# Splitting the weights of the matmul stage on VectorE and ScalarE alone, with two load buffers held by both stages

## The chip, the core and the metric

The kernel runs on one core of a Trainium2 chip. TensorE (PE in the profile) does the matmuls, VectorE (DVE), ScalarE (ACT) and GpSimd (POOL) the elementwise work, and SyncE (SP) issues all loads and stores from one queue, in order. The metric is the device time of one execution in microseconds (us); lower is better.

## What is computed

The reference is an attention with a memory term, followed by two gated feed-forward layers:

```python
a = softmax(causal(q @ k.T / 8))
local = a @ v
mem_out = (phi(q) @ M_prev) / (phi(q) @ z_prev + 1e-6)     # phi(x) = elu(x) + 1
x = g * mem_out + (1 - g) * local                          # g = sigmoid(beta), per head
x = (sigmoid(x @ w_gate) * (x @ w_val)) @ w_out            # layer 0
x = ((x @ w_a) * (x @ w_b)) @ w_out2                       # layer 1
```

q, k, v are 4 x 8 x 576 x 64, so the layers see 2304 tokens of width 512; the hidden width is 1536. Inputs of the kernel and all weights are taken as float64 words: each weight arrives as two 32-bit halves.

## The kernel before

Every float32 operand of a matmul is kept as a high and a low part of type fp32r, and every product is three matmuls into one PSUM sum (`mm3`, lines 501 to 503: high by high, high by low, low by high). The hidden width is cut into 12 chunks (`NCH`) of 128. A chunk of a layer has three weight pieces, gate, value and output (`kind` 0, 1, 2), and each piece must be brought from 64-bit words into a high and a low tile before TensorE can use it. `w_piece` does that for one piece: a load of 512 KB into a buffer `st`, then the split, in three steps between its `yield`s. `w_stream` runs pieces one behind the other and issues loads ahead.

The kernel has two stages. The first, to about 357 us of the profile, is the attention, with the layer-0 matmuls of chunks 0 to 3 (`MA`) for three of the four batches woven in (`moe_a`); it also splits the 15 pieces of chunks 0 to 4 (`KA`). A scheduler orders the instructions of all engines there. The second is the matmul stage. There TensorE's order is the program's; the other engines are still ordered by the scheduler. `run` goes over the chunks of one block of tokens: for chunk c, `gv` does 24 matmuls (gate and value sums), then 12 matmuls of the chunk before, `outs`, follow. Between them lies `gate`: DVE multiplies (L579, it reads PSUM), ACT writes the high part `gh` (L149), GpSimd the low part `gl` (L585), and `outs` of that chunk needs both. The blocks go in this order: layer 0, batch 3, all 12 chunks; layer 0, the 256 left-over tokens (blk = 4); layer 0, batches 0 to 2, chunks 4 to 11; then layer 1. Weight pieces are split under these blocks: 21 pieces (chunks 5 to 11 of layer 0) under the first, 12 pieces of layer 1 under batch 0, 24 under batch 2 and the first block of layer 1. `w_steps(k)` runs k steps of the stream at each chunk, placed behind the last gate instruction by `tc.issue_after`.

In the matmul stage a piece costs DVE six instructions (L415, L419, L420, L434, L439, L448), ACT one (L416) and GpSimd one multiplication (L424), which stands between them: L439 reads what L424 writes. Three buffers `st` take the loads, in memory that the first stage gives back.

Of the kernel before, what the change touches and what calls it, by code (L numbers as in the profile page):

```python
# [12 lines left out]
ALU = mybir.AluOpType  # L13
# [6 lines left out]
def kernel(  # L20
# [38 lines left out]
    wp = ctx.enter_context(tc.tile_pool(name="wp", bufs=KA))  # L59
    xsp = ctx.enter_context(tc.tile_pool(name="xsp", bufs=4))  # L60

    lctx, rctx = ExitStack(), ExitStack()
# [338 lines left out]
    def w_piece(wsrc, layer, c, kind, src):  # L401
        s = work.tile([P, 512, 2], I32, tag="st", name="st", bufs=NST)
        w32 = wsrc[kind].bitcast(I32)
        if kind == 2:
            nc.sync.dma_start(out=s.rearrange("p f t -> p (f t)"), in_=w32[c * P:(c + 1) * P, :])
        else:
            nc.sync.dma_start(
                out=s.rearrange("p (a f) t -> p a (f t)", a=KD),
                in_=w32[:, 2 * c * P:2 * (c + 1) * P].rearrange("(a p) f -> p a f", p=P),
            )  # L410
        yield
        hi, lo = s[:, :, 1], s[:, :, 0]
        top = work.tile([P, 512], I32, tag="wt", name="wt", bufs=NW)
        low = work.tile([P, 512], I32, tag="wl", name="wl", bufs=1)
        vec.tensor_scalar(out=top, in0=hi, scalar1=0x7FFFFE00, scalar2=None, op0=ALU.bitwise_and)  # L415
        act.activation(out=top, in_=top, func=AF.Relu, scale=8.0, bias=rebias)  # L416
        yield
        t = src.tile([P, 2, 512], F32R, tag=f"w{kind}", name=f"w{kind}")
        vec.tensor_scalar(out=low, in0=hi, scalar1=0x1FF, scalar2=None, op0=ALU.bitwise_and)  # L419
        vec.tensor_scalar(  # L420
            out=hi, in0=hi, scalar1=-(1 << 31), scalar2=0x3F800000, op0=ALU.bitwise_and,
            op1=ALU.bitwise_or,
        )
        pool.tensor_tensor(  # L424
            out=t[:, 0], in0=top.bitcast(F32), in1=hi.bitcast(F32), op=ALU.mult
        )
        if WPOOL:
            act.activation(out=low.bitcast(F32), in_=low, func=AF.Copy, scale=2.0 ** -20)
            vec.scalar_tensor_tensor(
                out=low.bitcast(F32), in0=lo.bitcast(U32), scalar=2.0 ** -52, in1=low.bitcast(F32),  # L430
                op0=ALU.mult, op1=ALU.add,
            )
        else:
            vec.scalar_tensor_tensor(  # L434
                out=low.bitcast(F32), in0=low, scalar=2.0 ** 32, in1=lo.bitcast(U32),
                op0=ALU.mult, op1=ALU.add,
            )
        yield
        vec.tensor_scalar(  # L439
            out=top, in0=t[:, 0].bitcast(I32), scalar1=-(1 << 23), scalar2=None,  # L440
            op0=ALU.bitwise_and,
        )
        if WPOOL:
# [3 lines left out]
        else:  # L447
            vec.scalar_tensor_tensor(  # L448
                out=t[:, 1], in0=low.bitcast(F32), scalar=2.0 ** -52, in1=top.bitcast(F32),
                op0=ALU.mult, op1=ALU.mult,  # L450
            )
        ws[layer, c, kind] = t
        yield

    def w_stream(pieces, ahead, skew=False):

        gens = []  # L460
        pieces = iter(pieces)

        def more():
            a = next(pieces, None)
            if a is not None:
                g = w_piece(*a)
                next(g)
                gens.append(g)

        for _ in range(ahead):  # L470
            more()
        yield
        old = None
        if skew and gens:
            next(gens[0])
            yield
        while gens:
            g = gens.pop(0)
            if skew:
                if old:  # L480
                    next(old)
                    yield
                if gens:
                    next(gens[0])
                    yield
                next(g)
                more()
                yield
                old = g
                continue  # L490
# [5 lines left out]
        if old:  # L496
            next(old)
            yield

# [232 lines left out]
    w1, w2_ = (w1g, w1v, w1o), (w2a, w2b, w2o)  # L732
    NST, NG, NW = 2, MA, 1
    CD = "q"
    EDVE = ""
    WPOOL = True
    if True:
        start()
        wst = w_stream(
            [(w1, 0, c, kind, wp) for kind in range(3) for c in range(MA)]  # L740
            + [(w1, 0, c, kind, wp) for c in range(MA, KA) for kind in range(3)], 2
        )
        batches = list(range(B - 1))
        cur, deferred, finished, cut_a = [], [], [], []
# [40 lines left out]
        def fill(p):  # L785
            settle()
            split(1)
            if p >= 1:
                with tc.issue_after(st["pace"].ins):
                    for _ in range(1 if p < 4 else 2):  # L790
                        next(wst, None)

        def room(p):

            old = divmod(p - 4, NPAIR)
            while any(x[1] is split_a and x[2] == old for x in split_q):
                split(1)
                if not M():
                    next(wst, None)

# [99 lines left out]
        while cur or batches or split_q or deferred:  # L900
            M()
            fill(NP)
        for _ in wst:
            pass
    rctx.close()
    lctx.close()
    with tc.manual_schedule(engines={mybir.EngineType.PE}):
# [5 lines left out]
        psb = bctx.enter_context(tc.tile_pool(name="psb", bufs=4, space=bass.MemoryType.PSUM))  # L913
        NST, NG, NW = 3, 2, 2
        WPOOL = False
        wst = w_stream(
            [(w1, 0, c, kind, w2) for c in range(KA, NCH) for kind in range(3)], NST, True
        )

        def w_steps(k):  # L920
# [30 lines left out]
        every, upper = list(range(NCH)), list(range(MA, NCH))  # L951
        run(0, B - 1, every, lambda m: w_steps(9), (0, B))
        w_steps(1000)
        run(0, B, every, lambda m: None, (0, 0))
        for blk in range(B - 1):
            last = blk == B - 2
            if blk == 0:
                wst = w_stream(
                    [(w2_, 1, c, kind, wp) for c in range(MA) for kind in range(3)], NST, True
                )  # L960
            if last:
# [4 lines left out]
                        for c in range(MA, NCH) for kind in range(3)  # L966
                    ], NST, True
# [39 lines left out]
```

## Time and profile before

| | |
|---|---|
| time, 3 runs | 1184.41, 1187.15, 1188.86 us; median 1187.15 |
| profiled execution | 1186.88 us, of which the span is 1185.1 |
| busy in the span | PE 1136.8, DVE 560.2, ACT 446.5, POOL 435.8 us |
| TensorE's granted clock | 0.991 of full on the mean |

The page cuts the span into 40 slices of 29.6 us and gives the busy tenths of each engine. In this kernel PE is at nine tenths or more from the sixth slice to the end, but for one place, the slices around 420 to 470 us. A busy share says little of a stage in which PE does all that it can; what matters here is where PE waits, and for whom.

### The profile page before, as it was taken

The numbers are of one execution on the slowest core, as the hardware profiler recorded it, in microseconds if no ns is written. First come the engines' busy times: TensorE is split into PE (matmuls) and PEld (weight loads), VectorE is DVE, ScalarE is ACT, GpSimd is POOL, SyncE is SP. The second block draws the span as 40 slices with busy tenths as digits, with TensorE's granted clock in tenths as the row PEclk, the third lists the DMA queues.
The fourth block names the chain that finished last, engine by engine and source line by source line (L and its number), as shares of the span: only waits on it lengthen the run. The fifth ranks groups of instructions, "written<-read, shape, count | busy, mean of one in ns | idle before, by whom it ended". The sixth has DMA issues, their size and how long they took to land. (4 is left out here: it accounts for less than half of the span.)

```text
span 1185.1 us, 16296 instructions
## 1 busy us (share of the span) xinstructions
PE 1136.8 (96%) x6088; PEld 928.6 (78%) x6088; DVE 560.2 (47%) x1233; ACT 446.5 (38%) x985; POOL 435.8 (37%) x387
## 2 busy tenths in 40 slices
PE   5889899999999987999999999999999999999998
PEld 4667677787878865998888887878888888888897
DVE  6899988655636776127721579741100200200111
ACT  5877767777743222132312223222211211211221
POOL 5777776453413553124421254431111111111111
PEclk9999999999999998999999999999999999999999
DMA  7454443342114333014420334401000200100000
GB/s 172 111 154 107 131 118 109 77 112 76 46 50 150 122 107 120 36 53 135 134 89 10 132 107 131 154 18 36 36 1 1 72 1 1 51 8 1 5 37 18
DMA packets 130816, 89.67 MB, mean 76 GB/s; under 512 B 90417, under 2 KB 118065, under 8 KB 129841
## 3 DMA queue, kind: packets, MB, share of 16 engines
q1 hardware_dynamic: 130736, 88.63, 25.9%
q8 instruction: 48, 0.79, 0.3%
q14 instruction: 32, 0.25, 0.1%
HBM read 71.31 MB, written 17.30 MB: 75 GB/s over the span
## 5 line engine op out<-in xcount | busy, mean ns | idle before, releaser
L585 POOL TENSOR_TENSOR gl<-sg,gh 128x512 fp32r<-128x512 f32 (+1 forms) x120 | 145.9, 1216 | 506.4 <-ACT gh L149 480.4
L501 PE MATMUL gv<-xs,w 128*128 128x512 f32 (+1 forms) x864 | 320.0, 370 | 5.8 <-POOL w L424 5.2
L503 PE MATMUL gv<-xs,w 128*128 128x512 f32 (+1 forms) x864 | 320.0, 370 | 3.3 <-DVE w L448 3.3
L502 PE MATMUL gv<-xs,w 128*128 128x512 f32 (+1 forms) x864 | 319.7, 370 | 1.6 <-DVE xs L644 1.6
L579 DVE TENSOR_TENSOR sg<-gv,sg 128x512 f32<-128x512 f32 (+1 forms) x108 | 68.1, 630 | 417.0 <-PE gv L503 408.0
L501 PEld LDWEIGHTS gv<-xs,w 128*128 128x128 f32 x864 | 163.5, 189 | 37.2 <-POOL w L424 7.0
L503 PEld LDWEIGHTS gv<-xs,w 128*128 128x128 f32 x864 | 163.6, 189 | 33.9 <-DVE w L448 5.3
L502 PEld LDWEIGHTS gv<-xs,w 128*128 128x128 f32 x864 | 163.5, 189 | 31.9 <-DVE xs L644 2.7
L424 POOL TENSOR_TENSOR w<-wt,st 128x512 fp32r<-128x512 f32 x72 | 114.6, 1591 | 120.2 <-ACT wt L416 59.2
L149 ACT ACTIVATE gh<-sg 128x512 fp32r<-128x512 f32 (+1 forms) x120 | 70.5, 588 | 215.1 <-DVE sg L579 215.0
L666 ACT ACTIVATE sg<-gv 128x512 f32<-128x512 f32 (+1 forms) x108 | 59.0, 547 | 238.9 <-PE gv L503 234.8
L416 ACT ACTIVATE wt<-wt,rebias 128x512 int32<-128x512 int32 x72 | 51.9, 723 | 128.4 <-DVE wt L415 128.3
L247 ACT ACTIVATE s<-s,mx 128x320 f32<-128x320 f32 (+3 forms) x128 | 78.0, 610 | 24.6 <-DVE mx L242 23.7
L698 PE MATMUL mo<-w,gl 128*128 128x512 f32 x216 | 85.2, 395 | 1.5 <-POOL gl L585 1.4
L696 PE MATMUL mo<-w,gh 128*128 128x512 f32 x216 | 84.9, 393 | 0.0
L697 PE MATMUL mo<-w,gh 128*128 128x512 f32 x216 | 84.8, 393 | 0.0
L149 ACT ACTIVATE aw<-tp 128x512 f32<-128x512 f32 (+1 forms) x144 | 70.5, 508 | 27.5 <-PE tp L328 23.0
L502 PE MATMUL mo<-gl,w 128*128 128x512 f32 (+1 forms) x192 | 70.5, 367 | 1.5 <-POOL gl L585 1.5
L242 DVE CUSTOM_DVE_ANT_0 s<-sc,mask 64x64 f32<-64x64 f32 (+4 forms) x144 | 62.2, 470 | 17.9 <-PE sc L217 17.7
L501 PE MATMUL mo<-gh,w 128*128 128x512 f32 (+1 forms) x192 | 70.2, 366 | 0.0
L503 PE MATMUL mo<-gh,w 128*128 128x512 f32 (+1 forms) x192 | 70.2, 366 | 0.0
L439 DVE TENSOR_SCALAR wt<-w 128x512 int32<-128x512 int32 x72 | 36.2, 502 | 48.5 <-POOL w L424 48.5
(108 smaller groups left out, 1814.8 us busy)
## 6 DMA issues: line engine op xcount, KB each, us to landing
st<-in_moe_w_out_dram SPq DMA_DIRECT2D x24, 512.0 KB, 3.6
kn<-in_k_dram SPq DMA_DIRECT2D x64, 128.0 KB, 2.8
st<-in_moe_w_gate_dram SPq DMA_DIRECT2D x12, 512.0 KB, 3.7
st<-in_moe_w_val_dram SPq DMA_DIRECT2D x12, 512.0 KB, 3.8
st<-in_moe_w_a_dram SPq DMA_DIRECT2D x12, 512.0 KB, 3.6
st<-in_moe_w_b_dram SPq DMA_DIRECT2D x12, 512.0 KB, 3.5
xd<-x SPq DMA_DIRECT2D x16, 288.0 KB, 2.7
qn<-in_q_dram SPq DMA_DIRECT2D x32, 128.0 KB, 2.8
```

Source lines behind the costliest of these rows:

```text
L149: act.activation(out=out, in_=src, func=AF.Copy)
L242: st["pace"] = vec.tensor_tensor_reduce(out=s, in0=sc[0:m, SC0[i]:SC0[i] + w], in1=mask[0:m, c:c + w], scale=1.0, scalar=BIG, op0=ALU.add, ...
L247: act.activation(out=o, in_=s, func=AF.Exp, scale=-1.0, bias=mx[0:m, i:i + 1], accum_out=sm[0:m, i:i + 1],)
L424: pool.tensor_tensor(out=t[:, 0], in0=top.bitcast(F32), in1=hi.bitcast(F32), op=ALU.mult)
L501: pe.matmul(o, lhsT=w[:, 0, ws_], rhs=xh, start=first, stop=False, skip_group_check=True)
L502: pe.matmul(o, lhsT=w[:, 0, ws_], rhs=xl, start=False, stop=False, skip_group_check=True)
L503: pe.matmul(o, lhsT=w[:, 1, ws_], rhs=xh, start=False, stop=last, skip_group_check=True)
L579: st["gate"] = vec.tensor_tensor(out=s[:, 0:n], in0=vps[:, 0:n], in1=s[:, 0:n], op=ALU.mult)
L585: pool.tensor_tensor(out=gl[:, 0:n], in0=s[:, 0:n], in1=gh[:, 0:n].bitcast(F32), op=ALU.subtract)
L696: pe.matmul(mo[f], lhsT=gh[:, t], rhs=w[:, 0], start=first, stop=False)
L697: pe.matmul(mo[f], lhsT=gh[:, t], rhs=w[:, 1], start=False, stop=False)
L698: pe.matmul(mo[f], lhsT=gl[:, t], rhs=w[:, 0], start=False, stop=c == NCH - 1)
```

## The change

The load buffers `st` get a pool of their own, `stp`, with two buffers, which lives through both stages. The weight stream of the first stage is not closed at its end: its list now holds the 21 pieces of chunks 5 to 11 too, and a counter (`left`) stops it after 46 steps, so that loads of the next two pieces are issued in the first stage, and the matmul stage goes on with the same stream. In the matmul stage GpSimd's multiplication is gone. The DVE instructions of a piece are now: **top** (L417, upper bits), **low** (L420, low bits), **low sum** (L446), **sign** (L452, one instruction that puts the sign bit to the rescaled top), **cut** (L456, the power of two, written into `st`) and **second** (L459, the low tile, which reads `st`). ACT has two: the rescaling (L418) and, new, a copy of `top` that writes the high tile (L455). The order of steps by pairs (`skew`) is gone, and `w_steps` takes 6 steps at a chunk where it took 9. The first stage's split is as before.

```diff
+    stp = ctx.enter_context(tc.tile_pool(name="stp", bufs=2))
...
-        s = work.tile([P, 512, 2], I32, tag="st", name="st", bufs=NST)
+        s = stp.tile([P, 512, 2], I32, tag="st", name="st")
...
-        t = src.tile([P, 2, 512], F32R, tag=f"w{kind}", name=f"w{kind}")
         vec.tensor_scalar(out=low, in0=hi, scalar1=0x1FF, scalar2=None, op0=ALU.bitwise_and)
-        vec.tensor_scalar(
-            out=hi, in0=hi, scalar1=-(1 << 31), scalar2=0x3F800000, op0=ALU.bitwise_and,
-            op1=ALU.bitwise_or,
-        )
-        pool.tensor_tensor(
-            out=t[:, 0], in0=top.bitcast(F32), in1=hi.bitcast(F32), op=ALU.mult
-        )
...
+        vec.scalar_tensor_tensor(
+            out=low.bitcast(F32), in0=low, scalar=2.0 ** 32, in1=lo.bitcast(U32),
+            op0=ALU.mult, op1=ALU.add,
+        )
+        yield
+        t = (src or w2).tile([P, 2, 512], F32R, tag=f"w{kind}", name=f"w{kind}")
+        vec.scalar_tensor_tensor(
+            out=top, in0=hi, scalar=-(1 << 31), in1=top, op0=ALU.bitwise_and, op1=ALU.bitwise_or
+        )
+        act.activation(out=t[:, 0], in_=top.bitcast(F32), func=AF.Copy)
+        vec.tensor_scalar(
+            out=hi, in0=top, scalar1=-(1 << 23), scalar2=None, op0=ALU.bitwise_and
+        )
+        vec.scalar_tensor_tensor(
+            out=t[:, 1], in0=low.bitcast(F32), scalar=2.0 ** -52, in1=hi.bitcast(F32),
+            op0=ALU.mult, op1=ALU.mult,
+        )
         ws[layer, c, kind] = t
         yield
...
-            + [(w1, 0, c, kind, wp) for c in range(MA, KA) for kind in range(3)], 2
-        )
+            + [(w1, 0, c, kind, wp if c < KA else None) for c in range(MA, NCH) for kind in range(3)],
+            2,
+        )
+        left = [1 + 9 * KA]
...
-        wst = w_stream(
-            [(w1, 0, c, kind, w2) for c in range(KA, NCH) for kind in range(3)], NST, True
-        )
...
-        run(0, B - 1, every, lambda m: w_steps(9), (0, B))
+        run(0, B - 1, every, lambda m: w_steps(6), (0, B))
...
-                    [(w2_, 1, c, kind, wp) for c in range(MA) for kind in range(3)], NST, True
+                    [(w2_, 1, c, kind, wp) for c in range(MA) for kind in range(3)], 2
...
-            run(0, blk, upper, (lambda m: 1 < m < 7 and w_steps(9)) if last else
+            run(0, blk, upper, (lambda m: 1 < m < 7 and w_steps(6)) if last else
...
-            run(1, blk, every, lambda m: w_steps(9), (1, order[i + 1]) if i < B else None)
+            run(1, blk, every, lambda m: w_steps(6), (1, order[i + 1]) if i < B else None)
```

TensorE's order of instructions is the same in both kernels, and so is the order on DVE, ACT and GpSimd in the whole first stage. Two places of the matmul stage differ in what the prediction rests on.

The first is DVE's queue in the first block, before. The rows begin with the gate of chunk 2 (`sg<-gv,sg`); twelve weight rows stand between it and the gate of chunk 3, of which eleven are shown (w_4750 and w_4763 are tiles of two pieces).

```order
L579 TENSOR_TENSOR sg<-gv,sg 128x512
L439 TENSOR_SCALAR wt<-w_4750 128x512
L448 SCALAR_TENSOR_TENSOR w_4750<-wl,wt 128x512
L415 TENSOR_SCALAR wt<-st 128x512
L419 TENSOR_SCALAR wl<-st 128x512
L420 TENSOR_SCALAR st<-st 128x512
L434 SCALAR_TENSOR_TENSOR wl<-wl,st 128x512
L439 TENSOR_SCALAR wt<-w_4763 128x512
L448 SCALAR_TENSOR_TENSOR w_4763<-wl,wt 128x512
L415 TENSOR_SCALAR wt<-st 128x512
L419 TENSOR_SCALAR wl<-st 128x512
L420 TENSOR_SCALAR st<-st 128x512
```

The same place after the change, from the gate of chunk 1 on (L568 is the gate now).

```order
L568 TENSOR_TENSOR sg<-gv,sg 128x512
L417 TENSOR_SCALAR wt<-st 128x512
L420 TENSOR_SCALAR wl<-st 128x512
L446 SCALAR_TENSOR_TENSOR wl<-wl,st 128x512
L452 SCALAR_TENSOR_TENSOR wt<-st,wt 128x512
L417 TENSOR_SCALAR wt<-st 128x512
L456 TENSOR_SCALAR st<-wt 128x512
L459 SCALAR_TENSOR_TENSOR w_4749<-wl,st 128x512
L452 SCALAR_TENSOR_TENSOR wt<-st,wt 128x512
L420 TENSOR_SCALAR wl<-st 128x512
L446 SCALAR_TENSOR_TENSOR wl<-wl,st 128x512
L456 TENSOR_SCALAR st<-wt 128x512
```

No row waits for GpSimd's tile any more (before, L439 reads `w`). Between two gates there now stand 14 weight rows, not 12: 5, 7, 14, 14, 13, 14, 14, 13, 14, 12 and 6 rows ahead of the gates of chunks 0 to 10. The last row of a piece (L459) frees its `st` for the load of the piece after the next.

The second place is SP's queue at the start of the matmul stage. Before, the first three pieces are loaded here, ahead of the loads `xt` of the left-over tokens:

```order
L407 DMA st<-in_moe_w_gate_dram 128x4x256
L407 DMA st<-in_moe_w_val_dram 128x4x256
L405 DMA st<-in_moe_w_out_dram 128x1024
L636 DMA xt<-xd_94 128x64
L636 DMA xt<-xd_95 128x64
```

After, the first two pieces have been loaded in the first stage, and the third stands behind ten loads `xt`, the last four of which are shown:

```order
L625 DMA xt<-xd_99 128x64
L625 DMA xt<-xd_100 128x64
L625 DMA xt<-xd_97 128x64
L625 DMA xt<-xd_98 128x64
L407 DMA st<-in_moe_w_out_dram 128x1024
L625 DMA xt<-xd_99 128x64
L625 DMA xt<-xd_100 128x64
L409 DMA st<-in_moe_w_gate_dram 128x4x256
```

The third piece has moved behind the ten small loads, and the first two are gone from here.

## Rows read from the trace of the kernel before

**Rows 1.** The page: its span, and the busy row of part 1.

```profile
span 1185.1 us, 16296 instructions
...
PE 1136.8 (96%) x6088; PEld 928.6 (78%) x6088; DVE 560.2 (47%) x1233; ACT 446.5 (38%) x985; POOL 435.8 (37%) x387
```

**Rows 2.** Windows: length, busy by engine, granted clock, DMA share, GB/s.

```profile
420.00:440.00 20.00, 17.78 (x75) 13.48 (x73) 14.81 (x28) 5.13 (x8) 10.54 (x7) 1.00 0.34 106
440.00:460.00 20.00, 12.27 (x42) 7.67 (x42) 15.99 (x29) 4.64 (x7) 9.24 (x6) 0.87 0.36 108
...
452.00:456.00 4.00, 1.04 (x3) 0.59 (x3) 3.36 (x5) 0.63 (x1) 2.82 (x2) 0.87 0.41 127
456.00:460.00 4.00, 1.80 (x4) 0.62 (x3) 2.73 (x7) 0.72 (x1) 1.66 (x1) 0.50 0.19 53
```

**Rows 3.** Waits of PE, 335 to 480 us: total, times, longest.

```profile
PE gv L501 <- POOL w L424: 5.2, 4, 2.2
PE gv L503 <- DVE w L448: 3.3, 3, 1.4
```

**Rows 4.** Timeline of PE: start, duration; first matmuls of three groups.

```profile
370.58 0.39 PE L501 MATMUL gv<-xs,w 128*128 128x512 f32 x1
...
378.74 0.39 PE L501 MATMUL gv<-xs,w 128*128 128x512 f32 x1
...
469.57 0.28 PE L501 MATMUL gv<-xs,w 128*128 128x256 f32 x1
```

**Rows 5.** Timeline of DVE, one round in the first block; idle time in brackets.

```profile
414.77 0.69 DVE L579 TENSOR_TENSOR sg<-gv,sg 128x512 f32<-128x512 f32 x1
...
416.52 1.67 DVE L448 SCALAR_TENSOR_TENSOR w<-wl,wt 128x512 fp32r<-128x512 f32 x1
418.22 0.43 DVE L415 TENSOR_SCALAR wt<-st 128x512 int32<-128x512 int32 x1
418.56 0.42 DVE L419 TENSOR_SCALAR wl<-st 128x512 int32<-128x512 int32 x1
419.02 0.43 DVE L420 TENSOR_SCALAR st<-st 128x512 int32<-128x512 int32 x1
419.36 0.69 DVE L434 SCALAR_TENSOR_TENSOR wl<-wl,st 128x512 f32<-128x512 int32 x1
421.25 0.43 DVE L439 TENSOR_SCALAR wt<-w 128x512 int32<-128x512 int32 x1 [1.20 <-POOL w L424]
421.71 0.69 DVE L448 SCALAR_TENSOR_TENSOR w<-wl,wt 128x512 fp32r<-128x512 f32 x1
422.44 0.43 DVE L415 TENSOR_SCALAR wt<-st 128x512 int32<-128x512 int32 x1
...
424.18 0.68 DVE L579 TENSOR_TENSOR sg<-gv,sg 128x512 f32<-128x512 f32 x1
```

**Rows 6.** Timelines of ACT and POOL behind the gate at 414.77.

```profile
415.55 0.63 ACT L149 ACTIVATE gh<-sg 128x512 fp32r<-128x512 f32 x1 [1.33 <-DVE sg L579]
...
416.26 1.38 POOL L585 TENSOR_TENSOR gl<-sg,gh 128x512 fp32r<-128x512 f32 x1 [0.23 <-ACT gh L149]
```

**Rows 7.** Loads: two rows of SP's timeline, and st's landings, 360 to 470 us.

```profile
360.74 0.38 SPq L407 DMA_DIRECT2D st<-in_moe_w_gate_dram  x1
...
362.26 6.13 SPq L636 DMA_DIRECT2D xt<-xd  x9
...
DMA to landing us min/median/max: 3.4/3.6/5.9
```

**Rows 8.** Windows of the later blocks, columns as in Rows 2.

```profile
520.00:600.00 80.00, 80.00 (x363) 65.71 (x362) 54.77 (x96) 25.20 (x42) 33.69 (x22) 1.00 0.39 119
...
716.00:796.00 80.00, 76.39 (x325) 60.23 (x324) 60.43 (x101) 21.79 (x35) 36.58 (x24) 1.00 0.34 106
```

**Rows 9.** A gate of layer 1, after the last piece is split.

```profile
798.94 0.69 DVE L579 TENSOR_TENSOR sg<-gv,sg 128x512 f32<-128x512 f32 x1 [7.67 <-PE gv L503]
```

**Rows 10.** Landings of st in the first stage, 150 to 210 us.

```profile
DMA to landing us min/median/max: 3.6/4.8/6.1
```

More of the change, by code (lines that the diff above doesn't have):

```diff
@@ L417, in w_piece @@
         yield
-        t = src.tile([P, 2, 512], F32R, tag=f"w{kind}", name=f"w{kind}")
         vec.tensor_scalar(out=low, in0=hi, scalar1=0x1FF, scalar2=None, op0=ALU.bitwise_and)
-        vec.tensor_scalar(
-            out=hi, in0=hi, scalar1=-(1 << 31), scalar2=0x3F800000, op0=ALU.bitwise_and,
-            op1=ALU.bitwise_or,
-        )
-        pool.tensor_tensor(
-            out=t[:, 0], in0=top.bitcast(F32), in1=hi.bitcast(F32), op=ALU.mult
-        )
-        if WPOOL:
+        if WPOOL:
+            t = src.tile([P, 2, 512], F32R, tag=f"w{kind}", name=f"w{kind}")
+            vec.tensor_scalar(
+                out=hi, in0=hi, scalar1=-(1 << 31), scalar2=0x3F800000, op0=ALU.bitwise_and,
+                op1=ALU.bitwise_or,
+            )
+            pool.tensor_tensor(
+                out=t[:, 0], in0=top.bitcast(F32), in1=hi.bitcast(F32), op=ALU.mult
+            )
             act.activation(out=low.bitcast(F32), in_=low, func=AF.Copy, scale=2.0 ** -20)
@@ L432, in w_piece @@
             )
[L433 to L436, printed above, removed]
-            )
[L438 to L441, printed above, removed]
-        )
-        if WPOOL:
+            yield
+            vec.tensor_scalar(
+                out=top, in0=t[:, 0].bitcast(I32), scalar1=-(1 << 23), scalar2=None,
+                op0=ALU.bitwise_and,
+            )
             pool.tensor_tensor(
@@ L446, in w_piece, with w_stream @@
             )
[L447 to L450, printed above, removed]
-            )
+            ws[layer, c, kind] = t
+            yield
+            return
+        vec.scalar_tensor_tensor(
+            out=low.bitcast(F32), in0=low, scalar=2.0 ** 32, in1=lo.bitcast(U32),
+            op0=ALU.mult, op1=ALU.add,
+        )
+        yield
+        t = (src or w2).tile([P, 2, 512], F32R, tag=f"w{kind}", name=f"w{kind}")
[3 more added lines that the diff above has]
+        act.activation(out=t[:, 0], in_=top.bitcast(F32), func=AF.Copy)
+        vec.tensor_scalar(
+            out=hi, in0=top, scalar1=-(1 << 23), scalar2=None, op0=ALU.bitwise_and
[3 more added lines that the diff above has]
+            op0=ALU.mult, op1=ALU.mult,
+        )
         ws[layer, c, kind] = t
         yield
-    def w_stream(pieces, ahead, skew=False):
+    def w_stream(pieces, ahead):
         gens = []
@@ L472, in w_stream @@
         yield
[L473 to L476, printed above, removed]
         while gens:
             g = gens.pop(0)
[L479 to L490, printed above, removed]
             for i in range(3):
@@ L495, in w_stream @@
                 yield
-        if old:
-            next(old)
-            yield
     def mm3(o, w, ws_, xh, xl, first, last):
@@ L732 @@
     w1, w2_ = (w1g, w1v, w1o), (w2a, w2b, w2o)
-    NST, NG, NW = 2, MA, 1
+    NG, NW = MA, 1
+    WPOOL = True
     CD = "q"
     EDVE = ""
-    WPOOL = True
     if True:
@@ L740, with w_next @@
             [(w1, 0, c, kind, wp) for kind in range(3) for c in range(MA)]
-            + [(w1, 0, c, kind, wp) for c in range(MA, KA) for kind in range(3)], 2
-        )
+            + [(w1, 0, c, kind, wp if c < KA else None) for c in range(MA, NCH) for kind in range(3)],
+            2,
+        )
+        left = [1 + 9 * KA]
+        def w_next():
+            if left[0]:
+                left[0] -= 1
+                next(wst)
         batches = list(range(B - 1))
@@ L790, in fill @@
                     for _ in range(1 if p < 4 else 2):
-                        next(wst, None)
+                        w_next()
         def room(p):
@@ L798, in room @@
                 if not M():
-                    next(wst, None)
+                    w_next()
         for b in range(B - 1):
@@ L902 @@
             fill(NP)
-        for _ in wst:
-            pass
+        while left[0]:
+            w_next()
     rctx.close()
@@ L913 @@
         psb = bctx.enter_context(tc.tile_pool(name="psb", bufs=4, space=bass.MemoryType.PSUM))
-        NST, NG, NW = 3, 2, 2
+        NG, NW = 2, 2
         WPOOL = False
-        wst = w_stream(
-            [(w1, 0, c, kind, w2) for c in range(KA, NCH) for kind in range(3)], NST, True
-        )
         def w_steps(k):
@@ L966 @@
                         for c in range(MA, NCH) for kind in range(3)
-                    ], NST, True
+                    ], 2
                 )
-            run(0, blk, upper, (lambda m: 1 < m < 7 and w_steps(9)) if last else
+            run(0, blk, upper, (lambda m: 1 < m < 7 and w_steps(6)) if last else
                 (lambda m: m and w_steps(5)), (1, B - 1) if last else (0, blk + 1))
```

## Prediction, made before the changed kernel ran

> **What bounds the kernel now.** I read the page first: TensorE is busy for 1136.8 of 1185.1 us [rows 1], so only the places where it waits, or runs at a low clock, can give time back. Windows of the matmul stage, read next, show two such places. From 420 to 460 us PE is busy for only 17.8 + 12.3 of 40 us, and from 456 us the granted clock is 0.50, the lower of its two levels [rows 2]. From 716 to 796 us it lacks 3.6 us at full clock; between them PE is full [rows 8]. The table of waits says for whom PE waits in the first place: the weights, both the part that GpSimd writes (L424, 5.2 us) and DVE's (L448, 3.3 us) [rows 3].
>
> What that place costs in all is read from PE's timeline. Chunk 2 begins at 370.58 and chunk 3 at 378.74: 8.16 us a chunk, 36 matmuls of 0.227 [rows 4]. At that pace chunk 11 would begin at 370.58 + 9 x 8.16 = 444.0, and the left-over block, 36 matmuls later, at 452.2. It begins at 469.57 [rows 4]: **17.4 us** late. That holds waits, the slow clock, and all else.
>
> Why the weights are late stands in DVE's timeline. From one gate to the next it takes 424.18 - 414.77 = 9.41 us [rows 5], against PE's 8.16, and in that round it splits two pieces. Of the 9.41, 1.20 is waiting for GpSimd's multiplication in one piece, 0.6 in the other (the gate ends at 415.46, and L448 starts at 416.52 with one instruction of 0.46 ahead of it), and one DVE instruction is stretched from 0.69 to 1.67 us [rows 5]: the one that runs while GpSimd works on the gate's low part, from 416.26 to 417.64 [rows 6]. So DVE loses 1.25 us per chunk on PE; a gate that starts t late is noticed only when t exceeds 8.16 less the 2.87 us from a gate's start to the end of its `gl` (414.77 to 417.64 [rows 5, 6]), that is 5.3 us.
>
> **The change, part by part.**
>
> *A piece on DVE.* It stays at six instructions. From start to start in the rows: top 0.34 (418.22 to 418.56), low 0.46 (to 419.02, the next one depends on it), low sum 0.60 (L434's 0.69 less the 0.09 by which rows overlap), cut 0.46 (as L439 to L448), second 0.73 (L448 to L415) [rows 5]. The sign instruction has no row: bounds are 0.34 (the cheapest row of DVE) and 1.67 (the dearest). Its nearest row is L448, the same operation on the same shape with two tensors: 0.73 with a dependent one behind it. Sum 3.32, say 3.3 us, without a wait for GpSimd.
>
> *ACT's new copy* is of gh's shape, 0.63 us [rows 6]; it lies beside DVE's cut and second instructions. It costs nothing as long as the next rescaling isn't late (a rival below).
>
> *A round.* The order puts 14 rows, 2 1/3 pieces, between two gates. That is 7.7, plus the gate 0.60, plus the stretch by `gl`, which stays: 1.67 - 0.69 = 0.98. **9.3 us, against PE's 8.16.** So DVE still falls behind, by 1.1 a chunk, but it does 2 1/3 pieces in it, and is done before the end.
>
> The Trainium skill, "SBUF — State Buffer", section "Who interferes with whom", says that a VectorE instruction with two SBUF inputs, or in a two-port mode, and a GpSimd one exclude each other, so that the second "fully blocks". By that the stretch could be the whole of `gl`, 1.38 [rows 6], in place of 0.98; the delay worked out below would be 6 x 0.4 = 2.4 us more and the time 1172.9. The rows show 0.98.
>
> *The start.* The first two pieces are already loaded. The third load stands behind ten `xt` loads in SP's queue. Nine of them took 6.13 us, so ten take 6.8 from about 360.7 on, where this queue began to move before; with 3.6 to landing [rows 7] the third piece can start at 371.1. Fourteen rows and one stretch later it is 379.8; gate 2 could have run at 376.0 (370.58 + 24 x 0.227 [rows 4]): 3.8 us late.
>
> *From there to the end.* From gate 2 to gate 8 the order has 82 rows, 13.7 pieces: 45.1 us, and six gates with stretch 9.5, together 54.6. PE needs 6 x 8.16 = 49.0. Lateness at gate 8: 3.8 + 5.6 = 9.4, of which 5.3 are free: PE loses **4.1 us** there, in small waits from chunk 5 or 6 on. After gate 9 only 6 rows are left, so the weights of chunk 11 are there in time and the long wait with its slow clock is gone. Gain in this place: 17.4 - 4.1 = **13.3 us**.
>
> *Two load buffers.* A `st` is free only after the last instruction of its piece; then 3.6 us pass until the next load has landed [rows 7]. In the order five rows of the other piece lie in between, about 2.9 us. So DVE waits 0.7 for a load where no gate falls in between, and not where one does (0.60 + 0.98 more than covers it). With 1 1/3 uncovered pieces in a round that is 0.9 a round at most, 5.6 over the six rounds: PE's loss would then be 9.7. The lower bound is nothing. I take nothing in the sum, because the stretch and the load wait can fall together, and keep both ends. At the other end (no stretch, no late start) the loss of 4.1 is nothing too.
>
> The Trainium skill, "DMA: Bandwidth & Descriptors", section "Anatomy of one DMA — SWDGE (gpsimd) path", fits a transfer by 2.0 us and its bytes at 436 GB/s: an estimate of 3.2 us for 512 KB, by which this wait would be 0.3. The trace has 3.6.
>
> *Layer 1's pieces.* Under batch 0, PE was full [rows 8] and stays so: at most 12 rows a chunk, 6.6 + 1.6 = 8.2 us, against a chunk of 8.36 (7.67 + 0.69 [rows 9]). In the last split the order has 12 rows a chunk, and twice 14: two rounds 0.9 too long, within the 5.3. In the changed order the subtractions for the next block's input no longer stand among weight rows. Of the 3.6 us missing from 716 to 796 [rows 8] I give back **3.3**; bounds 0 and 3.6.
>
> *The first stage.* Same order on every engine but SP, which gets two loads more, among the loads of q, k and v. They take 4.8 us each there [rows 10] and are hidden behind a pair's work (16 pairs of heads in some 357 us): 0, with bounds of 1 us either way.
>
> **Sum.** 13.3 + 3.3 = 16.6. The profiled execution took 1186.88, its span 1185.1 and 1.8 around it; the median of the runs is 1187.15, 0.3 above. **1170.5 us.** The sum's bounds: loads always waited for, and layer 1 gaining nothing, 17.4 - 9.7 = 7.7, that is 1179.5; all of both places back, 21.0, that is 1166.
>
> **Rivals.** *Load waits bind, or the clock falls once more* (gain 6 to 12, 1175 to 1181). Two buffers against three speak for it, and a slow spell like the one from 456 us, were it 8 us long (the row shows 4 of them at 0.50), costs 4 us; against it: PE's waits here would be 1 us or less, and before the clock was at 1.00 from 420 to 440 with 2.2 us of such waits [rows 2].
>
> *Slower: the loads set the pace.* A pair of pieces then takes a load and a piece in turn. Each us of a load beyond 3.6 costs up to 1 us a pair, over 8 pairs from chunk 2 on; the gain of 16.6 is gone at a load of about 5.7 us. First-stage landings reach 6.1 [rows 10]: at that, 3 us slower, 1190. Against it: in this stage loads have the queue nearly alone, with a median of 3.6 [rows 7].
>
> *ACT takes GpSimd's place: no change.* In ACT's queue the rescaling of the next piece stands behind the copy of the one before, and the copy behind a DVE instruction. If DVE waits 1 us a piece for it, 16 pieces eat the gain: 1187. Against it: ACT's work a chunk is 2 1/3 x 1.36 + 1.2 = 4.4 of 8.16 us, and the rescaling has low and low sum, 1.06 us, to hide its 0.7.
>
> *The change does not do what it says.* It names two pieces a chunk, and the order has 2 1/3. At just two, a round is 6.6 + 1.6 = 8.2, PE's own pace, and the loss of 4.1 would be mostly gone: 1167.
>
> **How the numbers follow.** Chances: the forecast, with PE losing up to 7 us in the first place (1166 to 1174), 0.60; load waits or a clock fall (1175 to 1181), 0.18; no change (1181 to 1193), 0.11; slower, 0.06; below 1166, 0.05. A measurement of this kernel tells about 0.5%, 6 us, from no change. So faster by more: 0.83; within: 0.11; slower: 0.06. The range from 1164 to 1180 leaves out the last two, most of "no change", and the tail of the second case.
>
> **What would show it.** GpSimd has no weight instruction after 360 us; a DVE round in the first block is 9 to 9.5 us with 14 weight rows, and the sign row 0.69 long; PE waits for `gl` in several pieces of 1 us or less around 405 to 435, not for weights; the left-over block begins near 456; 1.00 is granted throughout; from then on every block ends about 13 us earlier, and the last ones 16 to 17. I am wrong if DVE's rows show waits for `st` loads or for ACT of over 1 us in each round, if the sign row takes over 1 us, or if the first stage itself ends more than 1 us later.

## The result and the profile after

The changed kernel takes **1172.69 us** (median of 4 runs, 1170.62 to 1175.74), the kernel before, in the same rounds, 1187.58 (4 runs): a ratio of 0.988, 95% interval 0.985 to 0.991. A second series gave 1173.81 against 1187.24, 0.9885 (0.9869 to 0.9901). The forecast was 1170.5, 2.2 us below. Two slow executions of this study are in no comparison: one of the kernel of experiment 3 at 3564 us, about three times its others, and one of the kernel before at 1228 us.

The page after, in answer to [rows 1]: the same TensorE work in 12.8 us less, and GpSimd's busy time down by 95 us.

```profile
span 1172.3 us, 16189 instructions
...
PE 1136.2 (97%) x6088; PEld 932.6 (80%) x6088; DVE 563.3 (48%) x1233; ACT 479.8 (41%) x1042; POOL 340.5 (29%) x330
```

Windows after, columns as in [rows 2]. The slow clock from 456 us is gone: 1.00 in all rows. PE still lacks 2.2 us from 420 to 440, and 0.5 (before: 3.6) from 716 to 796.

```profile
400.00:420.00 20.00, 19.51 (x85) 15.54 (x84) 18.34 (x32) 8.86 (x14) 2.71 (x2) 1.00 0.46 137
420.00:440.00 20.00, 17.78 (x76) 13.70 (x75) 17.97 (x31) 8.73 (x15) 3.06 (x2) 1.00 0.40 126
440.00:460.00 20.00, 19.87 (x85) 15.59 (x84) 15.15 (x25) 8.91 (x17) 3.90 (x3) 1.00 0.41 126
716.00:796.00 80.00, 79.47 (x345) 64.33 (x344) 55.75 (x96) 28.75 (x47) 11.74 (x9) 1.00 0.32 100
```

PE's waits from 335 to 480 us after. The two rows of [rows 3], waits for weights, are gone. What is left is a wait for the gate's low part.

```profile
PE mo L491 <- POOL gl L574: 3.6, 4, 1.2
```

For where the time went, I divide each span by two marks on PE's timeline: the first matmul of the gate and value matrices (`gv`), and the first one of the left-over block, the first with 256 columns. First the kernel before (the second mark is in [rows 4]), then after.

```profile
356.95 0.40 PE L501 MATMUL gv<-xs,w 128*128 128x512 f32 x1
```

```profile
359.37 0.40 PE L490 MATMUL gv<-xs,w 128*128 128x512 f32 x1
...
461.41 0.28 PE L490 MATMUL gv<-xs,w 128*128 128x256 f32 x1
```

All profiles of this study, read in the same way, in us; a ratio is to the kernel before in the same series:

| kernel | 1st stage, to first `gv` | clock 0:180 | first block | left-over block to end | median | ratio to before (95%) |
|---|---|---|---|---|---|---|
| before | 356.95 | 0.98 | 112.6 | 715.5 | 1186.3 to 1187.6, by series | 1 |
| changed | 359.37 | 0.94 | 102.0 | 710.9 | 1172.7 | 0.988 (0.985–0.991) |
| changed, second series | 358.92 | 0.96 | 101.8 | 711.6 | 1173.8 | 0.9885 (0.987–0.990) |
| 1 new arithmetic alone | 358.30 | 0.96 | 101.7 | 716.6 | 1176.7 | 0.991 (0.9895–0.993) |
| 2 old arithmetic in the changed one | 355.94 | 0.99 | 110.1 | 715.3 | 1184.2 | 0.998 (0.997–0.999) |
| 3 third load buffer | 358.13 | 0.96 | 96.9 | 710.1 | 1166.8 | 0.983 (0.981–0.984) |
| 4 low part on DVE | 356.51 | 0.98 | 96.6 | 709.6 | 1164.7 | 0.982 (0.980–0.9835) |
| 4 again | 356.37 | 0.98 | 96.6 | 709.5 | 1164.8 | 0.981 (0.980–0.9825) |
| 5 both | 359.33 | 0.94 | 96.6 | 709.5 | 1166.8 | 0.983 (0.981–0.984) |
| 6 nine steps | 357.95 | 0.96 | 106.8 | 716.0 | 1179.1 | 0.994 (0.993–0.996) |
| 7 low part twice | 356.46 | 0.98 | 108.5 | 721.6 | 1190.7 | 1.004 (1.003–1.005) |
| 8 before, low part on DVE | 358.26 | 0.95 | 109.5 | 709.5 | 1177.5 | 0.992 (0.991–0.993) |

So 10.6 us come from the first block and 4.6 from what follows; the first stage gave 2.4 back in this profile. That last part goes with the granted clock of the first 180 us, whichever kernel it is: 0.99 and 0.98 stand beside starts of 355.9 to 357.0, 0.94 beside 359.4. The least that this block takes with this work of PE is 96.6: there PE waits for nothing (experiment 4). Measured by that, before lost 16.0 us in the block and the changed kernel 5.4; after the block the floor is 709.5, and they lost 6.0 and 1.4. Of these, 0.4 each lie at the very end, behind the last `gv` matmul, and the rest, 5.6 and 1.0, at the layer-1 place (experiment 4 as the measure, matmul by matmul).

What a round looks like now, on DVE's timeline from one gate to the next (compare [rows 5]):

```profile
410.68 0.68 DVE L568 TENSOR_TENSOR sg<-gv,sg 128x512 f32<-128x512 f32 x1
411.28 0.42 DVE L420 TENSOR_SCALAR wl<-st 128x512 int32<-128x512 int32 x1
411.61 0.69 DVE L452 SCALAR_TENSOR_TENSOR wt<-st,wt 128x512 int32<-128x512 int32 x1
412.22 1.79 DVE L446 SCALAR_TENSOR_TENSOR wl<-wl,st 128x512 f32<-128x512 int32 x1
...
417.32 0.69 DVE L459 SCALAR_TENSOR_TENSOR w<-wl,st 128x512 fp32r<-128x512 f32 x1
418.81 0.43 DVE L417 TENSOR_SCALAR wt<-st 128x512 int32<-128x512 int32 x1 [0.80 <-DMA st<-in_moe_w_val_dram]
...
420.22 0.69 DVE L568 TENSOR_TENSOR sg<-gv,sg 128x512 f32<-128x512 f32 x1
```

GpSimd's timeline has one instruction in that round:

```profile
412.18 1.28 POOL L574 TENSOR_TENSOR gl<-sg,gh 128x512 fp32r<-128x512 f32 x1 [8.30 <-ACT gh L151]
```

The 1.20 for GpSimd's product has no successor. Two losses are left in these 9.54 us: the row at 412.22, stretched by 1.1 while GpSimd makes `gl` (412.18 to 413.46), and 0.80 for a load. A round is hardly shorter than before, 9.28 us on the mean of six in place of 9.40 (gates 2 to 8), but it holds more: the six have 82 weight rows, 13.7 pieces, where before had 72, 12 pieces. A piece with its share of all else takes 4.1 us in place of 4.7. Over the whole block, DVE's table of waits (340 to 470 us) has 6.8 us for loads:

```profile
DVE wt L417 <- DMA st<-in_moe_w_gate_dram: 3.7, 4, 1.0
...
DVE wt L417 <- DMA st<-in_moe_w_val_dram: 1.8, 2, 1.0
...
DVE wt L417 <- DMA st<-in_moe_w_out_dram: 1.3, 3, 0.6
```

### The profile page after: what moved, and what is told of

Read it like the earlier page. It is cut to its first block, busy times and chain, and to the rows that moved or that the text cites. A ratio compares the mean times of both kernels' runs of the same rounds, so it can differ in the third digit from the quotient of the medians.

```text
span 1172.3 us, 16189 instructions
## 1 busy us (share of the span) xinstructions
PE 1136.2 (97%) x6088; PEld 932.6 (80%) x6088; DVE 563.3 (48%) x1233; ACT 479.8 (41%) x1042; POOL 340.5 (29%) x330
## 4 chain that ended last, share of the span: by engine, by line
PE 59%; DVE 5%; DMA 3%; issue 1%; POOL 0%; ACT 0%; POOLq 0%; DVEq 0%; ACTq 0%
PE gv L492 13%; PE gv L491 13%; PE gv L490 13%; PE mo L687 4%; PE mo L686 4%; PE mo L685 4%; PE mo L491 3%; PE mo L492 3%; PE mo L490 3%; DMA st<-in_moe_w_gate_dram 2%; DMA st<-in_moe_w_out_dram 1%; DVE w L459 1%; DVE wl L446 1%; DVE wt L417 1%; DVE st L456 1%; DVE wl L420 1%
## 5 line engine op out<-in xcount | busy, mean ns | idle before, releaser
L568 DVE TENSOR_TENSOR sg<-gv,sg 128x512 f32<-128x512 f32 (+1 forms) x108 | 68.0, 630 | 417.6 <-PE gv L492 413.0
L418 ACT ACTIVATE wt<-wt,rebias 128x512 int32<-128x512 int32 x72 | 51.6, 721 | 66.1 <-DVE wt L417 66.0
L219 PE MATMUL sc<-kh,qt 128*64 128x64 f32 (+1 forms) x168 | 54.1, 344 | 4.4 <-ACT s L249 1.9
L455 ACT ACTIVATE w<-wt 128x512 fp32r<-128x512 f32 x57 | 36.1, 633 | 48.2 <-DVE wt L452 48.0
```

The costliest lines, as they stand in the source:

```text
L568: st["gate"] = vec.tensor_tensor(out=s[:, 0:n], in0=vps[:, 0:n], in1=s[:, 0:n], op=ALU.mult)
```

## Experiments

Theory: GpSimd's multiplication stood in the chain of DVE, and taking it out is the gain; the 5.4 us still lost in the first block are DVE's lateness, to which waits for two load buffers and the `gl` stretch add. Rivals: loads that start before the stage, or the new interleaving with its smaller step count, bring the gain.

**1. The new arithmetic alone**, in the kernel before: its three buffers, its later loads, its interleaving and nine steps.

```
-        pool.tensor_tensor(
-            out=t[:, 0], in0=top.bitcast(F32), in1=hi.bitcast(F32), op=ALU.mult
-        )
...
+        vec.scalar_tensor_tensor(
+            out=top, in0=hi, scalar=-(1 << 31), in1=top, op0=ALU.bitwise_and, op1=ALU.bitwise_or
+        )
+        act.activation(out=t[:, 0], in_=top.bitcast(F32), func=AF.Copy)
```

> The kernel before with the new arithmetic of the matmul-stage split alone: three load buffers in that stage's own pool, their loads begun in that stage, the old interleaving of pieces. Theory (the gain comes from GpSimd's multiplication leaving VectorE's chain): the first full block loses little, since its rounds shorten from 9.4 to about 8.5 us; the left-over block begins 102 to 106 us after the first gate/value matmul, against 112.6 before and 102.0 after the whole change, and the time is 1170 to 1178 us. VectorE waits for a load under 2 us in that block in place of the 6.8 us after the whole change, but its first weight operation comes some 3 us later, because the loads start later. Rival (the gain comes from loads that start before the stage, in the shared buffers): 1183 to 1188 us, and the left-over block begins 110 us or more after the first matmul. Rival (the new interleaving brings it): the same 1183 to 1188, with PE waiting for weights of the value matrix.

The block takes 101.7 us: the arithmetic alone gives the whole 10.9 us there. DVE's first weight instruction comes 7.9 us after the first `gv` matmul (3.7 in the changed kernel), and its load waits sum to 5.7 us, not under 2. Nor did the rounds shorten to 8.5 us: they take 9.34, but the six from gate 2 to gate 8 hold 86 weight rows, so a piece takes 3.9 us in place of 4.7. But from the left-over block on nothing is gained. PE's waits from 640 to 820 us are:

```profile
PE mo L511 <- POOL gl L594: 1.2, 1, 1.2
PE gv L510 <- ACT xs L652: 1.1, 1, 1.1
PE gv L511 <- DVE xs L653: 1.0, 2, 0.6
```

So the rivals are wrong for the first block, and one of them may hold for the layer-1 place.

**2. The old arithmetic in the changed kernel**: the edit of experiment 1, undone in the changed kernel; shared buffers, early loads, six steps and the new interleaving stay.

> The changed kernel with the old arithmetic of the split, GpSimd's multiplication included; shared load buffers, early loads and the new interleaving stay. Theory: a round of two weights is again bound by VectorE and GpSimd in turn, at 9.4 us or more, and two buffers in place of three add load waits; the left-over block begins 112 to 118 us after the first gate/value matmul, time 1184 to 1194 us. Rival (early loads and shared buffers bring the gain): 1172 to 1177 us. Rival (the interleaving): 1172 to 1177 as well, told apart from the former by the kernel that has the new arithmetic alone.

1184.2 us, 110.1 in the block, where I had said 112 or more; a round takes 9.5 us. Early loads and interleaving without the arithmetic bring 3 us. PE waits for weights again (from 340 to 480 us):

```profile
PE mo L482 <- POOL gl L565: 4.2, 6, 1.0
PE gv L481 <- POOL w L426: 2.2, 1, 2.2
PE gv L483 <- DVE w L450: 0.8, 1, 0.8
```

DVE's waits for the product are only 2.4 us in this block, but GpSimd costs it the time anyway, by stretching: the 12 rows of L417 in six rounds have a mean of 1090 ns, against 425 in experiment 4.

**3. A third load buffer in the matmul stage** of the changed kernel, three loads outstanding:

```
+        if not WPOOL and st["n"] % 3 == 2:
+            s = work.tile([P, 512, 2], I32, tag="st2", name="st", bufs=1)
+        else:
             s = stp.tile([P, 512, 2], I32, tag="st", name="st")
```

> The changed kernel with a third load buffer in the matmul stage, and three loads outstanding there. Theory (what the first full block still loses, 6.8 us by the left-over block's begin, is VectorE's lateness, which the waits for loads add to): the waits of VectorE for a load fall from 6.8 us to under 2 us, the third load is issued some 4 us earlier, the largest lateness of VectorE falls by 4 to 6 us, and the time with it, to 1166 to 1170 us. Rival (the load waits stand in time that VectorE has, PE's loss comes from the late start of the stage or from the GpSimd subtraction): 1171 to 1174 us though the waits are gone.

1166.8 us (1165.0 to 1166.8). A second profile was taken:

> The kernel with a third load buffer once more, for a profile. Theory (lateness of VectorE, which the load waits add to): VectorE's waits for loads in the first full block fall from 6.8 us to under 2 us, its largest lateness falls from 12 us to 7 us, and the left-over block begins 97 to 98 us after the first gate/value matmul, against 102.0 in the changed kernel. Rival (the gain of that kernel comes from the first stage or from the layer-1 place): the left-over block still begins 101 us or more after that matmul.

The block takes 96.9 us. DVE's load waits are 2.4 us (three rows, of 340 to 470 us), a little over the 2 expected, and PE is busy for all of 340 to 480:

```profile
DVE wt L421 <- DMA st<-in_moe_w_val_dram: 1.4, 2, 0.8
...
DVE wt L421 <- DMA st<-in_moe_w_out_dram: 0.6, 1, 0.6
DVE wt L421 <- DMA st<-in_moe_w_gate_dram: 0.4, 2, 0.2
```

```profile
340.00:480.00 140.00, 140.00 (x738) 1.00 0.36 112
```

So two buffers in place of three, by the load waits that the prediction put at nothing and by a later start (gate 2 is 1.6 us less late here), cost PE 5.1 us of the changed kernel's 5.4. The scheduler's order moves a little with the edit (80 weight rows in the six rounds, not 82), and that share is not told apart.

**4. The low part on DVE** in the matmul stage, so that GpSimd does nothing there beside it:

```
-        pool.tensor_tensor(
+        (pool if WPOOL else vec).tensor_tensor(
             out=gl[:, 0:n], in0=s[:, 0:n], in1=gh[:, 0:n].bitcast(F32), op=ALU.subtract
```

> The changed kernel with the subtraction that makes the gate's low part moved from GpSimd to VectorE in the matmul stage: GpSimd then does nothing there beside VectorE. By the traces the subtraction on GpSimd stretches one VectorE operation in each round from 0.7 to 1.4 to 1.8 us (about 0.9 us), and takes 1.2 us itself between the gate's high part and the matmul. Theory (the stretch costs VectorE as much as the work moved): VectorE's round stays within 0.4 us of what it was, the wait of PE for the low part shortens, time 1168 to 1173 us. Rival (VectorE is the bound and the moved subtraction takes a full 1.0 us or more of it): each round 0.5 to 1 us longer, time 1175 to 1181 us.

1164.7 us, below the expected range, and a round is 0.7 us shorter, not within 0.4 of what it was. DVE has 108 instructions more, and its gates come sooner: gate 8 starts 71.6 us after the first `gv` matmul (428.14 on DVE's timeline), against 79.4 in the changed kernel (438.75). Not all of these 7.7 us are the stretch: 3.7 are there at gate 2 already, and the six rounds hold 78 weight rows here, not 82, since the order moves with the edit. DVE still waits 7.9 us for loads, and that costs nothing now. Windows of PE (length, busy, granted clock, DMA share, GB/s):

```profile
340.00:480.00 140.00, 140.00 (x747) 1.00 0.34 108
640.00:800.00 160.00, 160.00 (x694) 1.00 0.31 99
```

It was run again beside the changed kernel:

> The changed kernel as it is, for more times and a second profile beside the next kernel. The start of the first gate/value matmul was 356 to 359 us in all profiles so far, with the same program in front of it up to two loads: if the 2.4 us by which the first profile of the changed kernel was later is the clock of the first 180 us and not the change, this profile has another start, within 356 to 359 us, that goes with its granted clock there. The left-over block again 102 us after it, and 711 us from there to the end; time 1170 to 1175 us.

> The changed kernel with the gate's low part on VectorE once more, timed beside the changed kernel on one chip. Expected from its first times: 1164 to 1167 us, and 6 to 10 us under the changed kernel; the left-over block 96.6 us after the first gate/value matmul and PE without a wait from there to 1000 us. If the difference of the two kernels were one of chips, it would shrink to under 3 us here.

1173.81 and 1164.78 on one chip: 9.0 us, the faster one at a ratio to before of 0.981 (0.980 to 0.9825), and so the best version found, by a move of one instruction a gate. Of the two spans' difference, 9.8, the first block has 5.2, the rest 2.1, and the start 2.5, which goes with the clock. Whether these two programs differ in that clock by more than chance stays open; their order of work is the same there.

**5. Both edits.**

> The changed kernel with both: a third load buffer in the matmul stage, and the gate's low part on VectorE. With the low part on VectorE alone PE waited for nothing from 340 to 1000 us, with VectorE still waiting for loads. Theory (only lateness beyond what PE has free costs): the third buffer takes VectorE's load waits away and gives nothing more, 1163 to 1167 us. Rival (the two edits remove separate losses and add up): 1157 to 1161 us.

1166.8 us, with 96.6 and 709.5 in the two parts, as in experiment 4: once PE does not wait, a buffer more gives nothing. The two profiles differ by 2.8 us, and these lie in the first stage (359.33 at a clock of 0.94, against 356.51 at 0.98).

**6. Nine steps of the weight stream after a gate again**, in the changed kernel:

```
-        run(0, B - 1, every, lambda m: w_steps(6), (0, B))
+        run(0, B - 1, every, lambda m: w_steps(9), (0, B))
...
-            run(0, blk, upper, (lambda m: 1 < m < 7 and w_steps(6)) if last else
+            run(0, blk, upper, (lambda m: 1 < m < 7 and w_steps(9)) if last else
...
-            run(1, blk, every, lambda m: w_steps(6), (1, order[i + 1]) if i < B else None)
+            run(1, blk, every, lambda m: w_steps(9), (1, order[i + 1]) if i < B else None)
```

> The changed kernel with nine steps of the weight stream after a gate again, where it has six. The kernel with the new arithmetic alone lost as little in the first full block as the changed one (101.7 against 102.0 us to the left-over block), but took 716.6 against 710.9 us from there to the end. Theory (nine steps put too many weight rows ahead of the split of the next block's input, so that PE waits for that at the layer-1 place): first block within 1 us of the changed kernel, 714 to 718 us from there to the end, PE waits 2 us or more for the split input there, time 1175 to 1179 us. Rival (what that kernel lost there comes from its later loads or its interleaving, not from the count): 1171 to 1174 us.

The rest takes 716.0 us, as expected, with PE waiting for the split input three times (1.8 us in sum; I had said 2 or more) and the clock falling behind it. PE's timeline, then windows of PE (columns as in experiment 4):

```profile
717.60 0.50 PE L491 MATMUL gv<-xs,w 128*128 128x512 f32 x1 [0.31 <-DVE xs L633]
719.67 0.50 PE L491 MATMUL gv<-xs,w 128*128 128x512 f32 x1 [1.10 <-DVE xs L633]
723.01 0.79 PE L491 MATMUL gv<-xs,w 128*128 128x512 f32 x1 [0.42 <-DVE xs L633]
```

```profile
715.00:720.00 5.00, 3.58 (x13) 1.00 0.57 166
720.00:725.00 5.00, 4.58 (x11) 0.51 0.74 232
725.00:730.00 5.00, 5.00 (x20) 0.81 0.54 159
```

So at the layer-1 place it takes both, the new arithmetic and the six steps, and each bears on a wait of its own. With nine steps PE waits for the split input, until 731 us: that costs 3.3 us before, 5.1 in experiment 1 and 6.1 here, and nothing with six. With six steps and the old arithmetic (experiment 2) PE waits from 760 us on for the gate's parts, which costs 4.0 us, and 1.0 and 1.6 in the two profiles of the changed kernel. PE's waits in experiment 2, 640 to 820 us:

```profile
PE mo L678 <- POOL gl L565: 2.0, 3, 0.7
PE mo L676 <- ACT gh L151: 0.7, 2, 0.4
```

The first block was not within 1 us, as I had said, but 4.8 longer. In the other order a load is issued at 435.00, when its buffer came free, and lands for the row at 440.27; gate 8 is queued behind it:

```profile
440.27 0.43 DVE L417 TENSOR_SCALAR wt<-st 128x512 int32<-128x512 int32 x1 [2.73 <-DMA st<-in_moe_w_gate_dram]
440.61 0.69 DVE L459 SCALAR_TENSOR_TENSOR w<-wl,st 128x512 fp32r<-128x512 f32 x1
441.21 0.68 DVE L568 TENSOR_TENSOR sg<-gv,sg 128x512 f32<-128x512 f32 x1
```

**7. The subtraction twice on GpSimd**, the second into a tile that nothing reads:

```
+        if not WPOOL:
+            g2 = work.tile([P, 512], F32, tag="g2", name="g2", bufs=1)
+            pool.tensor_tensor(
+                out=g2[:, 0:n], in0=s[:, 0:n], in1=gh[:, 0:n].bitcast(F32), op=ALU.subtract
+            )
```

> The changed kernel with the subtraction for the gate's low part done twice on GpSimd in the matmul stage, the second time into a tile that nobody reads, so that no instruction waits for it. Theory (each such operation stretches one VectorE operation by about 0.9 us): VectorE's round grows from 9.3 to 10.0 to 10.4 us, the left-over block begins 109 to 114 us after the first gate/value matmul, time 1180 to 1190 us. Rival (the subtraction costs only by the moment at which the low part is ready for PE): 1171 to 1175 us.

1190.7 us, just above the expected range. The rows between gates are the same in number as in the changed kernel. From gate 2 (380.29) to gate 8 (441.76) a round takes 10.25 us, against 9.28 in the changed kernel (383.04 to 438.75): 0.96 for one instruction that nobody waits for. DVE's timeline, and GpSimd's below it, show two stretched rows where there was one:

```profile
412.40 1.77 DVE L446 SCALAR_TENSOR_TENSOR wl<-wl,st 128x512 f32<-128x512 int32 x1
414.09 1.52 DVE L456 TENSOR_SCALAR st<-wt 128x512 int32<-128x512 int32 x1
```

```profile
412.35 1.26 POOL L574 TENSOR_TENSOR gl<-sg,gh 128x512 fp32r<-128x512 f32 x1 [7.57 <-ACT gh L151]
413.58 1.73 POOL L579 TENSOR_TENSOR g<-sg,gh 128x512 f32<-128x512 f32 x1
```

The block is 6.4 us longer, less than expected, and the rest 10.7.

**8. The low part on DVE in the kernel before**, its split unchanged; the edit is that of experiment 4.

> The kernel before with one edit only: the subtraction for the gate's low part on VectorE in the matmul stage; the split of the weights keeps GpSimd's multiplication. Theory (the change pays because that multiplication leaves the chain of VectorE, and the subtraction's place is a loss of its own of about 1 us a round): the waits of VectorE for GpSimd's product, 10.8 us in six rounds, shrink but stay, the round goes from 9.4 to between 8.8 and 9.3 us, the left-over block begins 104 to 111 us after the first gate/value matmul, time 1176 to 1185 us. Rival (any one GpSimd operation less is enough, since then both engines fit in the 8.2 us of PE): the left-over block begins 97 to 99 us after that matmul, time 1165 to 1171 us.

1177.5 us. The rest takes 709.5, the floor: moving the subtraction gives back all that before lost at the layer-1 place, with nine steps and the old arithmetic. So what experiment 6 says of that place holds while the subtraction is GpSimd's. In the block the round came out shorter than I said, 8.4 us (379.73 to 430.26 for gates 2 to 8), but the six hold 66 weight rows, not 72: a piece takes 4.6 us, hardly less than the 4.7 before, and DVE's waits for the product in them went from 10.8 to 9.0 us. The block takes 109.5, because the weights themselves are late at its end. There one piece goes through DVE, GpSimd and DVE with nothing between. POOL's timeline:

```profile
451.31 1.60 POOL L424 TENSOR_TENSOR w<-wt,st 128x512 fp32r<-128x512 f32 x1 [3.53 <-DVE st L420]
455.49 1.60 POOL L424 TENSOR_TENSOR w<-wt,st 128x512 fp32r<-128x512 f32 x1 [2.58 <-DVE st L420]
```

PE waits 6.1 us for L424 and 1.3 for L448 behind it. So one GpSimd operation less was not enough for this block: with the multiplication in the chain a piece costs nearly what it did before.

## Why the prediction was right, and where its sizes were off

**The mechanism held.** GpSimd has no weight instruction after 360 us, the sign row takes 0.67 to 0.69 us (0.73 assumed with its gap), ACT made DVE wait once, for 0.8 (by its rescaling, L418, before the first copy), the clock stays at 1.00 from 355 to 1160 us, and PE's waits are for `gl`, in pieces of 1.2 us or less. Experiments 1 and 2 put the gain of the first block on the arithmetic. One sign failed beside the first stage's below: the left-over block began at 461.41, not near 456. That the time came within 2.2 us of the forecast is in part luck: the block gave 2.7 us less than forecast, layer 1 gave 1.3 more (0.6 in the second profile).

**Gain in the first block: 13.3 forecast, 10.6 measured.** Of the 2.7 us between them, 1.4 lie in the 17.4 that the place was said to cost. That took 8.16 us for every chunk, and the block without a wait has a pace of 8.30 ((96.6 - 13.6) / 10; 8.16 up to chunk 5, 8.37 behind it), so before lost 16.0. The other 1.3 are PE's loss, 5.4 in place of 4.1, and the step that was mis-sized there is "I take nothing in the sum" for the two load buffers. In the six rounds DVE waited 3.1 us for loads (the 6.8 are those of the whole block). That is within the bound of 5.6, but it is not nothing, because the waits did not fall together with the stretch. The forecast had 9.4 us of lateness at gate 8; on the pace of 8.30 from gate 2 (19.05 us after the first `gv`) DVE was 10.5 late at gate 8 and 11.0 at gate 9 (447.54). The six rounds took 55.7 us in place of 54.6, and two errors partly cancel in them: a piece cost 3.1 us, not 3.3 (55.7 less 3.1 of load waits, 3.6 of gates and 6.2 of stretch, over 13.7 pieces), and the loads cost the 3.1. The rule that 5.3 us of lateness are free held: 11.0 less 5.3 is 5.7, and PE lost 5.4; in experiment 3 the greatest lateness was 5.4 (gate 6 at 415.80) and PE lost 0.2, in experiment 4 it was 4.8 (gate 9 at 438.42), and PE lost nothing. The 3.2 us that the prediction works out for a load rest on a fit for transfers that GpSimd issues; SyncE issues these, and they landed in 3.4 to 5.3 us here, 3.6 in the median.

**The start** was nearly right in size, 4.6 us late at gate 2 against 3.8, for a wrong reason. The ten `xt` loads took 4.59 us, not 6.8. The third load went out at 369.54 because its buffer was released then, by a last row stretched to 1.61. SP's timeline and DVE's:

```profile
363.04 4.59 SPq L625 DMA_DIRECT2D xt<-xd  x10
369.54 0.33 SPq L407 DMA_DIRECT2D st<-in_moe_w_out_dram  x1
```

```profile
367.90 1.61 DVE L459 SCALAR_TENSOR_TENSOR w<-wl,st 128x512 fp32r<-128x512 f32 x1
369.54 0.43 DVE L420 TENSOR_SCALAR wl<-st 128x512 int32<-128x512 int32 x1
```

**Layer 1: 3.3 forecast, 4.6 and 3.9 measured.** The bound of 3.6 was the idle time of the window, but the place cost 5.6. As experiments 1, 2 and 6 show, it took the arithmetic and the step count together, for two different waits; I had seen both only as rows of an order.

**The stretch by `gl`** was taken over at 0.98 and measured 1.03: in six rounds the rows of L420, L446, L456 and L417 exceed their medians by 6.2 us in sum, beside 8.9 us of subtractions on GpSimd. The Trainium skill, "SBUF — State Buffer", section "Who interferes with whom", says that the second of the two "fully blocks". The rows agree with it: in all six rounds the stretched row starts while the subtraction runs (0.04 to 0.50 us after its start), and is longer by the time from its own start to the subtraction's end less 0.13 to 0.14. The row at 412.22 has 1.24 us to that end, and is 1.10 longer. So the whole of `gl`, which the prediction took as what a full block would cost, is too much: its own row at 416.52 has 1.12 us left to the end of `gl` at 417.64, and is 0.98 longer [rows 5, 6].

**The first stage** ended 2.4 us later, which I had named as a sign of being wrong. The table shows the same spread with kernels that have the early loads and kernels that don't (355.9 to 359.4 and 357.0 to 358.3), in the order of the clock; at 0.98 the kernels with early loads start at 356.4 to 356.5, the kernel before at 356.95. So no cost of the early loads shows; that the clock is the cause is read from this order, and was not tested. **Rivals:** the loads did bind in part, but the clock did not fall and they never set the pace; ACT took nobody's place.

## What to carry to other kernels

An elementwise instruction on GpSimd beside a busy VectorE is not free, even when nobody waits for it: here each held one VectorE row until it ended and cost VectorE 1.0 us, more than the 0.6 that the same work takes on VectorE itself (experiment 4, from the row's start to the next). A round's length says little without the number of rows in it: count pieces, not rounds. Lateness of an engine off the bottleneck costs only what exceeds the slack of its consumer, so work out that slack first; then a load wait of a few us is worth a buffer, or nothing. When a buffer is dropped, the load wait worked out for it belongs in the sum, unless the rows show what covers it.

## What the runs showed of the hardware

A stretched row of VectorE ended 0.28 to 0.56 us after the GpSimd instruction that it had started beside, whether it read one tensor (L420) or two (L446): from 360 to 460 us of both kernels and of experiments 1, 3 and 7 it was longer than its like by the time from its start to GpSimd's end, less 0.13 to 0.15. The gate of the kernel before, which reads PSUM, started beside the multiplication in nine rounds and kept its 0.68. TensorE's granted clock was 0.51, its lower level, from 720 to 725 us, among three waits of 0.3 to 1.1 us between 717 and 723 (experiment 6), while waits of up to 1.2 us for `gl`, one in a chunk, left it at 1.00 (the changed kernel, 420 to 440 us); behind two waits in one chunk, of 1.0 and 0.9 us, it was 0.70 from 425 to 430 us (experiment 7). Idle time understates a wait: before lost 5.6 us at the layer-1 place, of which 3.6 show as idle; a matmul behind a wait is listed with 0.50 us and its successor starts 0.33 later, where others have 0.39 and 0.23 (kernel before):

```profile
721.84 0.39 PE L503 MATMUL gv<-xs,w 128*128 128x512 f32 x1
722.07 0.39 PE L501 MATMUL gv<-xs,w 128*128 128x512 f32 x1
722.95 0.50 PE L502 MATMUL gv<-xs,w 128*128 128x512 f32 x1 [0.49 <-DVE xs L644]
723.28 0.40 PE L503 MATMUL gv<-xs,w 128*128 128x512 f32 x1
```
